# First loads of k, block sums and score order of a fused attention and expert kernel, rearranged

## The chip, the cores and the metric

The kernel runs on one core of a Trainium2 chip. The metric is device time in microseconds (us). Matrix products run on TensorE (PE in the profile, its weight loads PEld), elementwise work on VectorE (DVE) and ScalarE (ACT), loads with a cast and small memsets on GpSimd (POOL), stores and transposing DMAs are issued by SyncE (SP).

## The reference, cut to what matters

q, k and v are [4 batches, 8 heads, 768 positions, 64], all f32. Attention sees a window of 16 positions on either side, and beside it 24 blocks of 32 keys, each as one key (the maximum) and one value (the mean). What comes out is x [3072, 512] of a feed-forward layer with w_in [512, 2048] and w_out [2048, 512].

```
k_sum = k.reshape(B, H, nb, block, D).max(axis=3)
v_sum = v.reshape(B, H, nb, block, D).mean(axis=3)
scores_s = scale * einsum('bhsd,bhnd->bhsn', q, k_sum) + log(block)
scores_l = where(|i - j| < 16, scale * q @ k.T, -1e9)
a = softmax(concat([scores_l, scores_s]))
x = a @ concat([v, v_sum])
h = x @ w_in
out = (h * clip(h + 3, 0, 6) / 6) @ w_out
```

## The kernel before, in words

Products run in bf16. A batch's 768 positions are cut into 12 query tiles of 64, and each tile sees 96 window keys and the 24 block keys: 120 rows. The block maxima stand as columns WIN to KEYS of each key tile, the block sums of v as rows WIN to KEYS of each value tile (`vaug`). Heads go in four pairs, `p` or `c`. A batch has two halves of query tiles; half 0 is tiles 6 to 11. Each half becomes one tile `s` = 0 to 7 of the feed-forward layer, of 384 rows.

All work is written down as operations (`op`) with a name, an engine or a choice of engines, a cost, what they read and write, and a function that issues them. The string ORDER lists every operation in the order in which the plan places it, with the engine chosen (`:D` VectorE, `:A` ScalarE, `:P` GpSimd). `Plan.run` gives each a begin time by its costs, sorts by it and issues; so ORDER fixes the order of each engine's own queue. Names:

- K, Q, V, I, O: loads of k, q, v, w_in, w_out, all on GpSimd's queue, with the cast to bf16 in the DMA. For batch 0, `K01`, `K02`, `K00` are pair 1, pairs 2 and 3, pair 0 (L400); `Q00`, `Q01` the q of half 0, and `Q01w` that of half 1 (L419, L420).
- k0p (L510 to L545): .0 the TensorE transposes of pair p (L517), .1 VectorE's block maxima (L538), .2 and .3 the copies of the half 0 and half 1 key tiles out of PSUM, .4 the block columns (L544).
- q0p0, q0p1: transposes and copies of q; s0px: scores of pair p and half x (products L628, exp on ScalarE L637, mask product on VectorE L641). For half 0 the mask is added by a `cover` matmul instead (L617).
- h0cx: the halo, 32 rows of v copied beside each value tile (L464). u0c: block sums of pair c by 12 matmuls (L677) to a tile `vf`, .1 the copy out, .2 and .3 the spreads into `vaug` (L683).
- v00 to v02: values of half 0 by tile of 128 rows (L754 to L758), .2 and .3 the reciprocal (L833) and scaling (L837), .4 the transposes of x (L850), .5 their copy. v03: values of half 1 (L784 to L792), then transposes (L809) and copies.
- For batches 1 to 3: load_raw and VectorE's 32x32 transposes (batches 1, 2), load_nat and SP's transposing DMAs (batch 3); w: block maxima over a batch (L719); sb0 to sb5: scores of a sixth of the batch each (L658, L664, L666); ub: block sums of the batch by 48 matmuls (L694), a copy and eight spreads (L700); vb0, vb3: values of a half, after which a transposing DMA on SP's queue (L797) makes x.
- F: first feed-forward product (L868), relu6 (L874, L876); G: the second (L890), a copy and a store.
- c, z, e, f: constants (`idle`, identity `ident`, the masks `band`, `band3`, `bias`, `mask`, the indicator `ind`). `keep` (L980) fills TensorE's planned gaps early on with matmuls on `idle`.

GpSimd issues, before: K01, K02, Q01's first load, `band` (c.2), the other, `ident` (c.1), K00, three wide q loads, four v loads, then w_in with batch 1's k. SP's queue has nothing before the first stores and the first transposing DMA of batch 1.

Of the kernel before, what the change touches and what calls it, by code (L numbers as in the profile page):

```python
# [15 lines left out]
D = 64  # L16
# [13 lines left out]
K01.0 K02.0 Q010.0 c.2 Q000.0 c.1 K00.0 k01.0 c.0 e.4 z2.0:D c.9 e.1 f.0 e.2 c.4 c.7 c.8 e.0 k01.1 k01.3:D z0.0:A z1.0:A  # L30
k02.0 k02.2:A z3.0:A k01.2:A e.3 k02.1 q020.0 q030.0 s020.0 q020.1:D k03.0 q030.1:D k02.4 s020.1 k02.3:A s030.0 k00.0 q000.0
k03.1 k03.4 s020.2 k00.2:A k03.2:A k03.3:A Q01w0.0 Q01w2.0 Q01w1.0 q010.0 s030.1 k00.1 q010.1:D q011.0 q021.0 q000.1:D k01.4
s030.2 k00.3:A q011.1:A q021.1:D q031.0 q031.1:D s031.0 s031.1 V00.0 h001.0:D V02.0 c.3 c.5 s031.2 V01.0 s011.0 s021.0 s021.1
s011.1 V03.0 q001.0 s010.0 u02.0 u00.0 u02.1:A h020.0:A I0.0 h000.0:D k00.4 I2.0 K13.0 I3.0 K10.0 K11.0 K12.0 s010.1 s000.0
s010.2 q001.1:A s000.1 u01.0 s001.0 u01.1:A u02.2:D u00.1:D u00.2:D h010.0:D h030.0:D h011.0:D h021.0:D s021.2 h031.0:D
u01.3:D s011.2 s000.2 u01.2:A u03.0 u03.1:A s001.1 v00.0 v00.1 v00.2 u03.2:A u00.3:A v02.0 v02.1 v01.0 v01.1 v00.3 s001.2
v00.4 v01.2 v01.3 v03.3 v03.0 v02.2 v02.3 v03.1 v03.4 v03.2 v03.5 v00.5:A v01.4 v01.5:A F00.0 F00.1 v02.4 F00.2 F00.3 F00.8
F00.9 v02.5:A F00.4 v03.6 F00.5 F00.10 F00.11 F00.12 F00.6 F00.13 v03.7:D v03.8 F02.0 F00.14 F00.7 c.6:D F00.15 F02.1 F02.2
F02.3 F02.4 v03.9:A F02.5 v03.10 v03.11:D F02.6 F02.7 F03.4 F03.5 F03.6 F03.7 F10.0 F10.1 F12.4 F12.5 F10.2 F03.0 F03.1 F12.6
k13.0 F10.3 F12.7 F03.2 F12.0 F12.1 F13.4 F13.5 k11.0 F03.3 I1.0 O0.0 Q13.0 Q10.0 O1.0 Q12.0 Q11.0 O2.0 O3.0 V13.0 V12.0  # L40
V10.0 V11.0 F12.2 F13.6 F12.3 k12.0 F13.7 F10.4 F10.5 F10.6 k10.0 F10.7 F01.0 F01.1 F01.2 F01.3 w1.0 F01.4 G02.0 F01.5 F01.6
F11.4 F11.0 F11.1 F11.5 F01.7 w1.1 w1.4:A F11.6 F11.7 F11.2 F11.3 q11.0 q13.0 q12.0 q10.0 w1.3:A w1.2:A G01.0 G01.1 F13.0
# [27 lines left out]
G61.1 G61.2 G71.6 G71.9 G61.3 G71.10:D G71.1 G71.4 G71.7 G71.12 G61.4:D G71.11 G61.5 G71.13:A G71.14  # L70
"""

BANKS = ("S", "h")


SLOW = 5.8
# [155 lines left out]
def kernel(  # L232
# [161 lines left out]
    def low(x):  # L394

        return (1 - x) * HQ
# [629 lines left out]
```

## Time and profile before

| | us |
|---|---|
| median of 3 runs | 214.84 |
| lowest, highest | 214.73, 215.09 |
| the profiled execution's own time | 214.44 |
| its span | 212.7 |
| mean granted TensorE clock | 0.99 |

The span runs from the first to the last instruction of the profiled execution. "Busy" counts the time in which an engine has an instruction of its own in flight. A row such as `L538 DVE ... x4 | 3.8, 941 | 1.6 <-` reads: line 538, four instructions, 3.8 us busy, 941 ns each, 1.6 us idle ahead of them and what ended it. The chain of waits goes back from the last instruction: at each step to what released it. A merged row of the timeline (`x2`) gives the start of the first and the time to the end of the last.

### The profile page before, as it was taken

To read this page: it belongs to the slowest core of one execution; us is meant where nothing else is said; L and a number is where in the kernel's file an instruction comes from. 1 tells how busy PE (TensorE), PEld (TensorE's weight loads), DVE (VectorE), ACT (ScalarE), POOL (GpSimd) and SP (SyncE) were. 2 spreads that over 40 slices of the span, in tenths; PEclk is the share of its full clock that TensorE was granted. 3 is DMA by queue.
4 is the path that set the end of the run, shared out by engine and by line. 5 is a ranking of instruction groups with operands and counts; after the bars stand their busy time and mean duration, and the time that the engine had idled before them with its cause. 6 is when DMAs were issued, how large, how long until landed. Compare 5 with 4: busy or idle time off the path is not lost.

```text
span 212.7 us, 4928 instructions
## 1 busy us (share of the span) xinstructions
PE 205.3 (97%) x2105; PEld 116.8 (55%) x2105; DVE 149.8 (70%) x238; ACT 110.6 (52%) x157; POOL 66.9 (31%) x81
## 2 busy tenths in 40 slices
PE   7969999999999999999999999999999999999994
PEld 2447686655446555555555556555464555555462
DVE  5788988999978897898568679981874347542102
ACT  5478856658299036836893045669501246531120
POOL 7999247345420029945973000000000000000000
PEclk9988999999999999999999999999999999999999
DMA  4999999999999659999999999901109002000242
GB/s 64 184 157 194 179 135 177 147 149 184 151 115 47 176 123 103 143 210 153 162 148 143 136 190 171 208 0 52 51 3 197 0 3 99 0 0 3 99 159 89
DMA packets 121846, 25.01 MB, mean 118 GB/s; under 512 B 112864, under 2 KB 118880, under 8 KB 121824
## 3 DMA queue, kind: packets, MB, share of 16 engines
q0 software_dynamic: 102336, 14.47, 108.0%
q1 hardware_dynamic: 19488, 10.23, 20.4%
q8 instruction: 16, 0.26, 0.5%
q14 instruction: 6, 0.05, 0.1%
HBM read 28.93 MB, written 6.29 MB: 166 GB/s over the span
## 4 chain that ended last, share of the span: by engine, by line
PE 90%; DVE 6%; ACT 2%; issue 0%; ACTq 0%; DVEq 0%
PE S L868 39%; PE h L890 29%; PE S L890 11%; PE S L784 3%; PE h L983 2%; PE S L658 2%; DVE vaug L502 2%; ACT kb L502 1%; DVE xn L837 1%; DVE at L641 1%; DVE kb L544 1%; PE h L517 1%; PE S L694 1%; DVE q L502 1%; DVE red L538 0%
## 5 line engine op out<-in xcount | busy, mean ns | idle before, releaser
L868 PE MATMUL S<-x,win 128*128 128x384 bf16 (+1 forms) x544 | 88.3, 317 | 0.0
L874 ACT ACTIVATE r<-S 128x768 f32<-128x768 f32 x64 | 51.3, 811 | 67.2 <-PE S L868 65.6
L876 DVE SCALAR_TENSOR_TENSOR g<-r,S 128x768 bf16<-128x768 f32 x64 | 59.6, 948 | 26.8 <-ACT r L874 26.1
L868 PEld LDWEIGHTS <-win 128*128 128x128 bf16 x544 | 51.2, 98 | 34.8 <-issue 0.2
L890 PE MATMUL h<-wout,g 128*128 128x512 bf16 (+1 forms) x288 | 67.4, 370 | 0.0
L890 PEld LDWEIGHTS <-g 128*128 128x128 bf16 x416 | 38.4, 98 | 38.6
L890 PE MATMUL S<-wout,g 128*128 128x512 bf16 (+2 forms) x128 | 25.8, 346 | 0.0
L664 ACT ACTIVATE at<-S 120x1024 bf16<-120x1024 f32 x18 | 17.5, 1031 | 4.3 <-PE S L658 4.2
L453 POOL DMA_DIRECT2D vaug<-in_v_dram x16 | 15.2, 955 | 8.1 <-DMA wout<-in_moe_w_out_dram 4.3
L666 DVE TENSOR_TENSOR at<-at,mask 96x1024 bf16<-96x1024 bf16 x18 | 11.9, 685 | 7.4 <-ACT at L664 7.2
L442 POOL DMA_DIRECT2D nat<-in_q_dram x8 | 10.5, 1318 | 7.1 <-issue 7.1
L442 POOL DMA_DIRECT2D nat<-in_k_dram x8 | 10.7, 1348 | 5.0 <-issue 2.3
L502 ACT COPY ot<-h 128x512 f32<-128x512 f32 (+1 forms) x14 | 7.9, 567 | 7.3 <-PE h L890 5.2
L502 DVE COPY ot<-S 128x512 f32<-128x512 f32 (+2 forms) x6 | 3.5, 577 | 11.2 <-PE S L890 11.2
L719 DVE TENSOR_REDUCE red<-kb 128x48 bf16<-128x1536 bf16 x6 | 10.5, 1744 | 0.0
L502 DVE COPY vaug<-vs 24x768 bf16<-24x768 bf16 x17 | 6.0, 354 | 3.4 <-ACT vs L502 3.0
L784 PEld LDWEIGHTS <-at 120*64 120x64 bf16 x336 | 6.1, 111 | 2.7 <-issue 1.6
L983 PE MATMUL h<-g 128*128 128x512 bf16 x15 | 6.1, 566 | 1.5 <-DVE g L323 1.5
L792 DVE TENSOR_TENSOR xm<-S,rc 128x768 bf16<-128x768 f32 x8 | 7.5, 955 | 0.1
L596 DVE STREAM_TRANSPOSE kb<-nat 128x768 bf16<-128x768 bf16 x8 | 7.4, 957 | 0.0
L784 PE MATMUL S<-vaug,at 120*64 120x65 bf16 x336 | 7.0, 196 | 0.3 <-ACT vaug L502 0.3
L637 ACT ACTIVATE at<-S 120x768 bf16<-120x768 f32 x8 | 6.3, 818 | 1.8 <-PE S L628 1.7
(100 smaller groups left out, 161.4 us busy)
## 6 DMA issues: line engine op xcount, KB each, us to landing
out_dram<-ot SPq DMA_DIRECT2D x19, 256.0 KB, 2.5
vaug<-in_v_dram POOLq DMA_DIRECT2D x16, 192.0 KB, 8.0
win<-in_moe_w_in_dram POOLq DMA_DIRECT2D x4, 512.0 KB, 11.2
wout<-in_moe_w_out_dram POOLq DMA_DIRECT2D x4, 512.0 KB, 17.3
nat<-in_k_dram POOLq DMA_DIRECT2D x10, 192.0 KB, 13.1
nat<-in_q_dram POOLq DMA_DIRECT2D x10, 192.0 KB, 8.1
out_dram<-ot SPq DMA_DIRECT2D x4, 224.0 KB, 2.7
nat<-in_k_dram POOLq DMA_DIRECT2D x6, 128.0 KB, 7.0
```

What stands on the lines that cost most here:

```text
L442: op("POOL", 1.35, over=0.01, fn=lambda src=src, name=name, hs=hs, ds=ds, rows=rows: nc.gpsimd.dma_start(out=raw[b % 2][name][rows], in_=s ...
L453: op("POOL", 0.945, lambda: nc.gpsimd.dma_start(out=o[BLK:WIN, lo:hi, 0:D], in_=rows[:, lo:hi]), w=[("v", b % 2, c)], dma=1.28, els=1536)
L502: {"ACT": nc.scalar.copy, "DVE": nc.vector.tensor_copy, "POOL": nc.gpsimd.tensor_copy}[eng](o, i)
L664: op("ACT", 1.02, lambda: nc.scalar.activation(odds[0:KEYS, :, w], X.slot[0:KEYS], AF.Exp, scale=scl), r=[X], w=[("atg", k)])
L666: op("DVE", 0.69, lambda: nc.vector.tensor_tensor(odds[0:WIN, :, w].rearrange("p j (t c) -> p j t c", c=QB), odds[0:WIN, :, w].rearrange(" ...
L719: nc.vector.tensor_reduce(red.slot[:].rearrange("x (p u e n) -> x e u p n", p=NP, u=NS, e=2)[:, e], w[:, n * e:n * e + n, BLK:WIN].rearran ...
L784: nc.tensor.matmul(X.slot[64 * c:64 * c + 64, e, (D + 1) * y:(D + 1) * (y + 1)], at[p][0:KEYS, j, t * QB:(t + 1) * QB], vaug[b % 2][0:KEYS ...
L868: nc.tensor.matmul(h.slot[:, f, lo * 128:hi * 128].rearrange("p (u c) -> p u c", c=128), w_in_sb[:, kt, (ft + f) * 128:(ft + f + 1) * 128] ...
L874: op("ACT", 0.81, lambda: nc.scalar.activation(r.slot[:], h.slot[:, :, 0:HALF], AF.Relu, bias=0.5, scale=1.0 / 6.0), r=[h], w=[r], alloc=r)
L876: op("DVE", 0.955, lambda: nc.vector.scalar_tensor_tensor(gt[s].slot[:, ft:ft + 2], r.slot[:], 1.0, h.slot[:, :, 0:HALF], op0=ALU.min, op1 ...
L890: nc.tensor.matmul(bank(o)[:, a:z], gt[s].slot[:, ft, ts * 128:(ts + 1) * 128], w_out_sb[:, ft, a:z], start=(ft == 0), stop=(ft == NFT - 1))
L983: nc.tensor.matmul(o, idle[:, 0:128], idle[:], start=True, stop=True)
```

## The change

- K01 and K02 are issued on SP's queue as f32 into the space of a feed-forward tile, and rounded to bf16 by six copies C01, C02, C03 (.0 and .1, one per head) on ScalarE or VectorE. `band` and `ident` go ahead of GpSimd's loads, which now name `band` as something they read; the wide q loads come before K00.
- The block sums of batch 0 are made for two pairs at a time, (0, 2) and (1, 3), in two 32-row strips of one PSUM tile.
- The block sums of batch 3 no longer come from TensorE: v is loaded again in rows of one block each (`B3c`, four loads), and four VectorE reductions add 32 rows (`U3.0` to `.3`), a copy and the same eight spreads follow.
- A score group belongs to one half of the batch, and the values of a half wait for three groups, not six.
- x of half 1 of batch 1 (`v13`) goes by TensorE's transposes and three copies, as in batch 0, not by SP's transposing DMA.
- Halos and spreads may run on GpSimd: ORDER puts h020, h001, h030, h010, h031 and u02.1 there, and eight spreads and two halos of later batches. The block columns k0p.4 may run on ScalarE.
- The mask table gets eight more tiles, and its first part is shorter. Where the plan sees a gap of TensorE and no free PSUM, the `cover` matmul of half 0 is repeated.
- ORDER is new throughout. The head of it, and the part with batch 3's sums, are shown.

```
+K01.0 K02.0 c.2 c.1 Q010.0 Q000.0 Q01w2.0 Q01w1.0 Q01w0.0 c.0 z2.0:D e.1 f.0 c.9 e.3 c.7 c.4 C01.1:D e.2 C01.0:D c.8 z3.0:A
+z1.0:A z0.0:A k01.0 C02.1:A C02.0:A q030.0 q030.1:A C03.1:A K00.0 V02.0 V00.0 k02.0 s020.0 q020.0 k01.2:D C03.0:D k01.1 k02.1
+k01.4:D k01.3:A k03.0 q010.0 k03.2:A k02.2:A q010.1:A k02.3:A q020.1:D k03.1 k03.3:A k03.4:A q000.0 q000.1:D k02.4:D e.4
+q001.0 q031.0 q021.0 s020.1 q031.1:D q021.1:D e.0 s031.0 s020.2 s031.1 k00.0 s021.0 q011.0 q011.1:A s021.1 V03.0 V01.0
+q001.1:D k00.1 k00.2:D h021.0:D h000.0:D s011.0 s011.1 k00.4:A s030.0 s010.0 s030.1 s010.1 s000.0 s000.1 s030.2 s010.2 s000.2
+I0.0 I1.0 h020.0:P c.3 c.5 s031.2 s021.2 h001.0:P I3.0 h030.0:P I2.0 u00.0 u00.1:A u02.0:A k00.3:D s011.2 u00.2:D u00.3:D
+u01.0 s001.0 h010.0:P u02.1:P h031.0:P O0.0 K10.0 K12.0 K13.0 O2.0 K11.0 Q12.0 Q10.0 O1.0 Q11.0 Q13.0 u03.0:A u01.1:A s001.1
+u03.1:A h011.0:A u01.2:D u01.3:D s001.2 v00.0 v00.1 v01.0 v02.0 v01.1 v02.1 v00.2 v00.3 v00.4 v01.2 v01.3 v02.2 v02.3 v03.3
+v03.0 v03.1 v00.5:A v01.4 v01.5:D v02.4 F00.0 F00.1 F00.2 F00.3 v02.5:A F00.4 F00.5 v03.2 v03.6 v03.7:A F00.6 v03.4 v03.5
...
+F40.1 F23.2 F23.3 v23.4 v23.5 k3e1.0 q3x0.0 v23.6 q3x1.0 G31.5 G22.2 G20.3 F41.0 F43.4 F43.5 F40.2 G20.4:A F43.6 F40.3 U3.3
+G20.5 w3.1 F43.7 U3.2 w3.3:D F40.4 F41.1 F40.5 G21.0 w3.2:A F40.6 F41.2 F40.7 F41.3 F42.4 F42.5 F42.6 F42.7 w3.4:A G21.1
+G21.2 G21.3 s340.0 s340.1 s330.0 s350.0 G22.3 G21.4:A s350.1 F42.0 F42.1 U3.1 U3.4:A s330.1 F42.2 u3.2:A s330.2 u3.0:D F42.3
+F41.4 F41.5 F41.6 u3.5:P F41.7 G42.0 F43.0 F43.1 F43.2 s350.2 F43.3 F50.0 F50.1 F50.4 F50.2 F50.5 u3.6:A F50.6 F50.3 F52.4
+F52.5 F52.6 s340.2 F50.7 F52.7 G22.4:A G30.5 G21.5 G22.5 G42.1 G42.2 G42.3 s310.0 s300.0 s320.0 s320.1 G42.4:A s310.1 s300.1
+G40.0 G40.1 G40.2 F53.0 F51.4 s310.2 h30.0 V32.0 y10.0 h31.0 V33.0 V31.0 u3.3:P V30.0 h32.0 u3.7:P u3.1:P F53.1 F51.5 G41.0
+G41.1 G41.2 F53.2 F51.6 s300.2 F53.3 s320.2 u3.4:D F51.7 v33.0 v33.3 v30.0 G41.3 v33.1 v33.4 v33.2 v33.5 G41.4:D F53.4 F53.5
...
+    def load_wide_k(b, lo, hi):
+        plan.at(f"K{b}{lo}")
+        def raw_(p, n):
+            at_ = 2 * (p - 1) * RUN * D
+            return hards[0][0:RP].rearrange("p f c -> p (f c)").bitcast(F32)[:, at_:at_ + n * RUN * D].rearrange("p (h s d) -> p h s d", h=n, s=RUN)
+        op("SP", 0.4, lambda: nc.sync.dma_start(out=raw_(lo, 2 * (hi - lo)), in_=k[b, 2 * lo:2 * hi].rearrange("h (p s) d -> p h s d", s=RUN)),
+           w=[("kf", p) for p in range(lo, hi)], dma=0.95 * (hi - lo), kind="load")
+        for p in range(lo, hi):
+            plan.at(f"C{b}{p}")
+            for j in range(2):
+                op(EITHER, {"ACT": 0.59, "DVE": 0.68}, lambda eng, p=p, j=j: copy(eng, knat[:, 2 * p + j], raw_(p, 2)[:, j]),
+                   r=[("kf", p)], w=[("kn", p, j)])
...
     def scores_all(b, k):
-        X, n = Buf("S"), 8
-        of = sorted({i // NQ for i in range(n * k, n * k + n)})
+        X, n, half = Buf("S"), 8, 1 - k // 3
+        first = n * (k % 3)
+        of = sorted({i // HQ for i in range(first, first + n)})
...
+    def vsum_first(cs):
         T = Buf(("h", "S"))
         def mms():
             for t in range(NQ):
+                for i, c in enumerate(cs):
+                    nc.tensor.matmul(bank(T)[BLK * i:BLK * i + BLK, 0:2 * D], ind[:, t], vaug[0][0:WIN, 2 * c:2 * c + 2, t, 0:D],
+                                     start=(t == 0), stop=(t == NQ - 1))
...
+    def load_blocks(b, c):
+        plan.at(f"B{b}{c}")
+        op("POOL", 0.8, lambda: nc.gpsimd.dma_start(out=rows_v(b, c), in_=v[b, 2 * c:2 * c + 2].rearrange("h (n r) d -> n h (r d)", r=BLK)),
+           w=[("vb", b, c)], dma=0.95, els=192, free=[(n, 0, g) for n in ("Kr", "Qr") for g in range(4)])
+    def sum_blocks(b):
...
+                    x = both[0][:].rearrange("p u m -> p (u m)")[:, h * BLK * D:(h + 1) * BLK * D].rearrange("p (r d) -> p d r", r=BLK)
+                    nc.vector.tensor_reduce(total[:, h * D + lo:h * D + lo + n], x[:, lo:lo + n], axis=AX.X, op=ALU.add)
...
-            op("PE", 0.395, mms, form="values", r=([("atg", k) for k in range(6)] if b else [("at", p, half) for p in range(NP)])
+            op("PE", 0.395, mms, form="values", r=([("atg", 3 * (1 - half) + k) for k in range(3)] if b else [("at", p, half) for p in range(NP)])
...
-        if b:
+        if b > 1 or b and not half:
             op("SP", 1.3, lambda: nc.sync.dma_start(out=xt[s].slot[:].rearrange("p u k c -> p (u k) c"), in_=xm.slot[:], transpose=True),
...
+            elif o.again:
+                todo += [o.again] * int(max(o.begin - 0.15 - end, 0.0) / 0.33)
```

171 lines of the change are left out of this document (97 added, 74 removed).

## The prediction

> **What bounds the kernel now.** I read the page first (span, busy shares, the 40 slices), then the chain of waits, then the busy windows of the stages that the chain marks out.
>
> ```profile
> span 212.7 us, 4928 instructions
> ...
> PE 205.3 (97%) x2105; PEld 116.8 (55%) x2105; DVE 149.8 (70%) x238; ACT 110.6 (52%) x157; POOL 66.9 (31%) x81
> ...
> PE   7969999999999999999999999999999999999994
> ```
>
> TensorE (PE) is busy nearly everywhere; only the first slices and the last fall below 9. The chain says where it takes over:
>
> ```profile
> 28.14 0.15 DVE rc L791
> 28.29 0.60 PE S L868 x8
> ...
> 30.23 0.22 PE h L809 x4
> ...
> 95.92 0.86 PE h L890 x4
> 96.78 0.65 PE S L868 x4
> ...
> 117.44 0.78 PE S L694 x48
> ```
>
> ```profile
> 6.75:28.14 21.39, 18.56 (x385) 12.63 (x383) 19.47 (x46) 16.54 (x32) 17.30 (x20) 0.92 1.97 175
> 28.29:209.68 181.39, 181.37 (x1696) 102.12 (x1696) 126.71 (x176) 90.96 (x121) 44.21 (x47) 1.00 1.25 112
> 209.68:212.70 3.02, 0.00 (x0) 0.00 (x0) 0.00 (x0) 0.27 (x1) 0.00 (x0) 0.89 0.34 116
> ```
>
> The columns are the stretch, its length, the busy time of PE, PEld, DVE, ACT and POOL, the granted clock, the DMA share and GB/s. So there are three stages. The **head**, to 28.29 us, is batch 0's attention: VectorE is busy 19.47 of 21.39 us and ScalarE (ACT) 16.54, and TensorE waits for them. The **stream** is 181.39 us in which TensorE never stops; only TensorE work added, removed or starved counts there. The **tail** of 3.02 us is the last copy and store.
>
> The sum is made against the profiled execution: span 212.70, its own time 214.44, so 1.74 lies around the span. The median of the runs, 214.84, is 0.40 above that execution; I subtract differences from the median.
>
> **Stream.** Leaving out the block sums of batch 3 on TensorE removes one L694 group, 0.78 us. Turning x of half of batch 1 on TensorE adds three groups like L809's, 3 x 0.22 = 0.66. ORDER also puts the third x transposes of the first half (v02.4, now inside the stream, again 0.22 by L809's like) ahead of F00.0: 0.22 leaves the stream and enters the head. Stream: 181.39 - 0.78 + 0.66 - 0.22 = 181.05, a gain of 0.34. The pairwise sums of batch 0 issue the same 48 matmuls, in the head, where TensorE is not last; scores by halves issue the same 96 a batch. Both are worth nothing by themselves: they loosen what values must wait for. The x copies of that half (three, on ScalarE and VectorE, for one DMA transpose by SP) and the larger mask copy on ScalarE stand beside the stream, in which ScalarE is busy 91 of 181 us; they cost nothing. The repeated cover matmuls of the head only fill planned gaps of TensorE.
>
> What replaces the batch 3 sums is four VectorE reductions of 1024 elements a row. Nearest row:
>
> ```profile
> L719 DVE TENSOR_REDUCE red<-kb 128x48 bf16<-128x1536 bf16 x6 | 10.5, 1744 | 0.0
> ...
> L502 DVE COPY vaug<-vs 24x768 bf16<-24x768 bf16 x17 | 6.0, 354 | 3.4 <-ACT vs L502 3.0
> ```
>
> ```profile
> 122.70:143.00 20.30, 20.30 (x121) 11.55 (x118) 17.69 (x25) 12.24 (x16) 0.00 (x0) 1.00 0.78 142
> 143.00:160.00 17.00, 17.00 (x260) 9.49 (x260) 10.11 (x18) 8.29 (x10) 0.00 (x0) 1.00 0.09 33
> ```
>
> 1024/1536 of 1.744 is 1.16, times four 4.7 us; six of batch 3's eight spreads leave VectorE, 6 x 0.354 = 2.1. Net 2.6 us more, in two windows where VectorE idles 37.30 - 27.80 = 9.5 us under TensorE's stream: nothing. GpSimd (POOL) issues nothing there now and its DMA share is low, so the four block loads are hidden as well. If that cover went, each late us of VectorE would be one of TensorE.
>
> **Head, the start.** Pairs 1 to 3 of k now come by SP's queue as f32 and are cast by six copies, and the constants go ahead of GpSimd's loads.
>
> ```profile
> 5.38 0.29 POOL L318 TENSOR_SCALAR_AFFINE_SELECT ident<-ident 128x128 bf16<-128x128 bf16 x1
> ...
> 5.90 0.85 PE L517 MATMUL h<-ident,nat 96*64 96x96 bf16 x16
> ...
> 6.80 0.96 DVE L538 TENSOR_REDUCE red<-h 128x24 bf16<-128x768 bf16 x1 [0.72 <-PE h L517]
> ...
> 13.48 1.54 POOL L487 DMA_DIRECT2D win<-in_moe_w_in_dram  x2
> ```
>
> ```profile
> win<-in_moe_w_in_dram POOLq DMA_DIRECT2D x2, 512.0 KB, 9.3
> ...
> nat<-in_k_dram POOLq DMA_DIRECT2D x3, 192.0 KB, 5.0
> ```
>
> ```profile
> out_dram<-ot SPq DMA_DIRECT2D x19, 256.0 KB, 2.5
> ```
>
> ```profile
> SPq L1010 <- PEq L1010: 0.8, 1, 0.8
> ```
>
> ```profile
> L502 ACT COPY x<-h 128x512 bf16<-128x512 bf16 x2 | 1.2, 586 | 0.8 <-PE h L850 0.8
> ```
>
> The first k transposes start at 5.90, just after ident (5.67). Afterwards ident is early, and k waits for a load and two casts. SP is free at 0.8. No SP load stands in this trace; from issue to landing I bound it by SP's stores (2.5) and GpSimd's k loads (5.0): k lands at 3.3 to 5.8. A cast of 96x512 costs between 0.35 (the bf16 spread above) and 0.59 (ScalarE); I take 0.6, two make 1.2, and the transposes start at 4.5 to 7.0. The middle is today's start, so I take **no gain at the start**, 1.2 us either way. Nothing else is queued on SP then: its first store comes in the stream. The five early casts fall into time in which VectorE and ScalarE wait today.
>
> GpSimd's queue is reordered as well: the wide q loads go ahead of pair 0's k, and four halos stand between the chunks of w_in. Today the first chunk is issued at 13.48 and lands 9.3 us later, at 22.8; F00.0 needs it near 27, so up to 4 us of delay there are hidden. The other chunks follow it by the 2 us of two copies each, while F00 and F01 give TensorE over 5 us (eight groups of 0.65): hidden.
>
> **Head, VectorE's load** from its first reduction (6.80) to the third scaled tile (before the L791 that starts at 28.14), after which F00.0 starts:
>
> ```profile
> L538 DVE TENSOR_REDUCE red<-h 128x24 bf16<-128x768 bf16 x4 | 3.8, 941 | 1.6 <-ACT kb L502 0.9 <-PE h L517 0.7
> L502 DVE COPY q<-S 128x384 bf16<-128x384 bf16 x6 | 2.7, 485 | 0.1
> L544 DVE COPY kb<-red 128x288 bf16<-128x288 bf16 x4 | 2.6, 646 | 0.1
> L641 DVE TENSOR_TENSOR at<-at,mask 96x768 bf16<-96x768 bf16 x4 | 2.2, 552 | 0.4 <-ACT at L637 0.4
> L837 DVE TENSOR_TENSOR xn<-S,rc 128x512 bf16<-128x512 f32 x3 | 2.1, 692 | 0.1
> L502 DVE COPY vaug<-vaug 32x640 bf16<-32x640 bf16 x4 | 1.5, 380 | 0.0
> L502 DVE COPY vaug<-g 24x768 bf16<-24x768 bf16 x3 | 1.5, 484 | 0.1
> L502 DVE COPY vaug<-vaug 32x768 bf16<-32x768 bf16 x3 | 1.2, 412 | 0.0
> ...
> L502 DVE COPY kb<-h 128x480 bf16<-128x480 bf16 x1 | 0.6, 648 | 0.0
> ```
>
> These rows and the small ones between (short halos 0.7, two small k copies 0.4, mask 0.7, reciprocals 0.6, a cast 0.3, a memset 0.1) add to 21.0 us, and the stretch took 21.3: overlaps and waits nearly cancel. The new ORDER gives VectorE, from k01.2 to v02.3: four maxima 3.76, one cast 0.6, two first-half k copies and one second-half (0.75 + 0.75 + 0.9) 2.4, two block columns 1.29, five q copies 2.43, two memsets 0.3, two halos 0.96, the shorter mask 0.4, four mask products 2.2, four spreads 1.94, three scalings with reciprocals 2.7: **19.0 us, 2.1 less**. Out are four halos and a spread (to GpSimd), one halo and some copies (to ScalarE); in are k copies and a cast. ScalarE's own list comes out about even: three casts (1.8) and a halo for two long k copies, one halo, two spreads and a tile copy.
>
> The 2.1 us is an upper end. Two equally loaded engines hand work to each other more often, and v00.0 now also waits for halos from GpSimd's queue, behind its loads; I charge 0.9, within bounds of 0 and 2.1. VectorE's end: 28.1 - 1.2 = 26.9. Then F00.0 waits for v02.4 (0.22 and a handover), 27.3 against 28.29: a **head gain of 1.0**.
>
> Sum: 1.0 + 0.34 = 1.3 us. Span 211.4, and **214.84 - 1.3 = 213.5 us**.
>
> **GpSimd's copies.** Six copies of the head move there: five halos and a spread. No GpSimd copy of that size stands in the trace; 0.36 to 0.83 (VectorE, ScalarE) bound one, and I take 0.83, 5 us in all. The trace shows what GpSimd does to VectorE:
>
> ```profile
> 15.16 0.23 DVE L544 COPY kb<-red 128x288 bf16<-128x288 bf16 x1
> ...
> 18.64 1.16 DVE L544 COPY kb<-red 128x288 bf16<-128x288 bf16 x1
> ```
>
> ```profile
> L442 POOL DMA_DIRECT2D nat<-in_k_dram x4 | 5.4, 1380 | 0.0
> ```
>
> One and the same copy took 0.23 us and 1.16, both beside GpSimd's issuing. The means above hold this loss already (0.646 against 0.23 four times is 1.7 us). The six copies displace 5.4 us of L442 issuing (it stands at 15 to 21 us now), so I charge nothing more; the other end is that every GpSimd copy holds VectorE up for its whole length, 5 us.
>
> [...]
>
> **Rivals.**
> - *The copies collide.* VectorE's mask products, halos and spreads stand exactly beside GpSimd's six copies. If each GpSimd copy holds VectorE for half its length, 6 x 0.42 = 2.5 us more: 214.84 - 1.3 + 2.5 = **216.0**. It turns the sign beyond 0.22 us a copy. For it: 1.16 against 0.23. Against: equal GpSimd work stands there now. [...]
> - *The head stays as long.* k lands late (5.0 rather than 2.5 us) and the casts stand on the way, or GpSimd's halos come late: the head gain is 0 and **214.5** is left.
> - *Batch 3 comes late.* Its v loads now queue on GpSimd behind a spread that needs all four reductions. Twelve instructions there, at the 0.83 taken above, are 10 us, against some 20 us of stream work that ORDER puts between (16 groups of 0.65, 10 of 0.86). Were VectorE 12 us late, TensorE would stop for 2: **215.5**.
> - *All of it counts.* k lands at 3.3 and waits do not grow: 2.1 + 0.34 and 0.2 at the start: **212.2**.
>
> **How the numbers follow.** Forecast (212.9 to 214.4) 0.45; more 0.16; head as long, 0.14; collision 0.16; batch 3 or another bubble 0.09. About 0.2%, 0.43 us, is what can be told from no change here. Faster 0.61, same 0.14, slower 0.25. The range runs from the large gain to the collision: 212.0 to 216.2.
>
> **What would show it.** F00.0 (first L868) near 27.3; the first L517 between 4.5 and 7; TensorE full from F00.0 to the end in about 181 us; no L694 group in batch 3; four reductions near 1.16 us. Wrong, if halos or mask products on VectorE in the head take much over 0.36 and 0.55 us, if SP's first load lands after 5.8, or if TensorE idles at batch 3's values.

## The result, and the profile after

The changed kernel takes 217.06 us (median of 4 runs, 216.84 to 217.39) against 214.80 (4 runs, 214.73 to 215.09): a ratio of 1.0104, interval 1.0086 to 1.0121. It is 1% slower, where 213.5 was forecast, and lies above the range. The profiled execution took 217.04 us, 2.60 more than the one of before (214.44), and its span is 2.62 longer: 215.33 against 212.71.

The page of the changed kernel, the same lines as of before:

```profile
span 215.3 us, 4890 instructions
...
PE 202.9 (94%) x2071; PEld 114.8 (53%) x2071; DVE 155.5 (72%) x225; ACT 112.7 (52%) x165; POOL 81.6 (38%) x102
...
PE   7869799999997999999899999999999999999992
```

The row of TensorE has a 7 and an 8 in the middle, in the slices from 64.6 and from 102.3 us: TensorE, which never stopped there before, now waits. The busy windows by the same three stages, with the columns of the prediction:

```profile
6.75:26.98 20.23, 16.11 (x389) 10.75 (x387) 18.21 (x40) 15.87 (x35) 16.79 (x24) 1.00 1.72 186
26.98:211.47 184.49, 181.58 (x1659) 102.10 (x1656) 132.55 (x169) 92.97 (x125) 58.83 (x65) 1.00 1.31 112
211.47:215.33 3.86, 0.00 (x0) 0.00 (x0) 0.00 (x0) 0.27 (x1) 0.00 (x0) 0.82 0.25 87
```

The head ends at 26.98 and not at 28.29, 1.31 us earlier. The stream takes 184.49 us and not 181.39, 3.10 more, with TensorE busy for 181.58 of it. The tail takes 3.86 and not 3.02. Together -1.31 + 3.10 + 0.84 = 2.63, the whole difference. So the gain came in the head, where most of it was forecast, and the loss in the stream, which was forecast 0.34 shorter, and in the tail, which was to stay as it was. TensorE's waits in the stream of the changed kernel, of which the kernel before has none:

```profile
PE h L753 <- ACT ot L528: 1.4, 1, 1.4
PE S L688 <- DVE g L941: 0.6, 1, 0.6
PE S L688 <- ACT kb L528: 0.5, 1, 0.5
PE S L849 <- DVE at L696: 0.3, 1, 0.3
PE S L874 <- DVE qwide L857: 0.2, 1, 0.2
```

The rows are ordered by length; in order of time the waits stand at 66, 70, 75, 106 and 130 us (1.35, 0.33, 0.15, 0.58 and 0.47). Each costs more than its idle time. The wait at 106 has 0.58 us of idle time, yet the groups of scores around it start 0.75 us later than their undisturbed distance; undisturbed, a group starts a little before the one ahead of it has ended (one of 0.87 us is followed after 0.81).

**The wait at 66 us** is for room to write to. The chain of waits there:

```profile
59.95 1.09 ACT ot L528 x2
...
61.05 4.65 DMA out_dram<-ot
...
65.80 0.59 ACT ot L528
...
66.44 0.88 PE h L753 x48
```

Output tiles leave PSUM through three `ot` buffers. The new ORDER finishes four tiles close together (G02, G01, G11, G10), and the first store took 4.65 us to land. ScalarE's copy of the fourth tile waits for that, and TensorE's block sums of batch 1 (L753) wait for the bank that this copy frees. Before, three such copies stood at 60 to 69 us and a fourth at 74.

**The wait at 106 us** comes from VectorE. Its timeline in the changed kernel, and then GpSimd's:

```profile
101.66 0.69 DVE L696 TENSOR_TENSOR at<-at,mask 96x1024 bf16<-96x1024 bf16 x1 [2.11 <-ACT at L694]
102.36 2.17 DVE L528 COPY vaug<-vs 24x768 bf16<-24x768 bf16 x3
104.57 0.69 DVE L696 TENSOR_TENSOR at<-at,mask 96x1024 bf16<-96x1024 bf16 x1
105.18 0.94 DVE L941 SCALAR_TENSOR_TENSOR g<-r,S 128x768 bf16<-128x768 f32 x1
```

```profile
102.60 1.72 POOL L528 COPY vaug<-vs 24x768 bf16<-24x768 bf16 x2
```

Three spreads took 2.17 us where one took 0.354 before (the row L502 of the prediction); two of them came while a GpSimd copy was running and took 0.88 each. The product at 105.18, which frees TensorE's next bank, stands behind them.

**The wait at 130 us** is for ScalarE's copy of k; the theory is that a VectorE that is full holds it up. VectorE's groups in the stream:

```profile
L740 DVE TENSOR_REDUCE total<-nat 128x32 f32<-128x1024 bf16 x4 | 7.7, 1918 | 0.0
...
L528 DVE COPY vaug<-vs 24x768 bf16<-24x768 bf16 x9 | 5.5, 611 | 0.2
```

A reduction takes 1.918 us, not the 1.16 of the forecast, and a spread 0.611 in the mean, not 0.354. What the waits at 70 and 75 us come from was not taken apart.

**The tail.** SP's waits at the end, first before and then after:

```profile
SPq L1021 <- DMA out_dram<-ot: 0.5, 2, 0.3
```

```profile
SPq L1094 <- DMA out_dram<-ot: 1.3, 1, 1.3
```

Before, SP waits for the two last stores last. After, one wait ends it, and others still follow. The trace's record of SP's closing instructions shows why (start in us; the semaphores each waits for):

```
before                              after
210.78 wait 115, 100                212.16 wait 112, 111
211.25 wait 116, 99                 213.47 wait 101, 110  <- last store landed at 213.46
211.59 wait 117, 107                213.53 wait 104, 109
211.79 wait 118, 109  <- 211.78     213.60 wait 113, 108
211.87 drain                        213.69 wait 114, 107
                                    213.77 wait 115, 106
                                    214.26 wait 116, 105
                                    214.34 wait 117, 100
                                    214.40 wait 118, 103
                                    214.48 drain
```

SP's transfers use eight semaphores in turn (111 to 118 before; 101, 104 and 113 to 118 after), and in both traces the closing waits go through these in the same order. With 40 transfers the last one falls on the last semaphore; with 41 it falls on the first, and seven waits come behind its landing: 1.02 us from landing to drain in place of 0.09. Of the 1.02, 0.48 is a single pause ahead of the wait for 116; before, a pause of 0.48 at the same place passed while the last stores were still under way.

### The profile page after: what moved, and what is told of

Same layout as the page of the kernel before. It is cut to its first block, busy times and chain, and to the rows that moved or that the text cites. A ratio compares the mean times of both kernels' runs of the same rounds, so it can differ in the third digit from the quotient of the medians.

```text
span 215.3 us, 4890 instructions
## 1 busy us (share of the span) xinstructions
PE 202.9 (94%) x2071; PEld 114.8 (53%) x2071; DVE 155.5 (72%) x225; ACT 112.7 (52%) x165; POOL 81.6 (38%) x102
## 4 chain that ended last, share of the span: by engine, by line
PE 69%; DVE 17%; DMA 5%; ACT 4%; issue 1%; SPq 0%; DVEq 0%; ACTq 0%
PE S L933 33%; PE h L955 22%; PE S L955 8%; DVE vaug L528 4%; DMA g<-in_k_dram 3%; DVE total L740 2%; DVE g L941 2%; DMA out_dram<-ot 2%; PE S L849 2%; DVE at L696 2%; DVE qwide L857 2%; ACT kb L528 2%; DVE red L783 2%; PE S L688 1%; ACT ot L528 1%
## 5 line engine op out<-in xcount | busy, mean ns | idle before, releaser
L941 DVE SCALAR_TENSOR_TENSOR g<-r,S 128x768 bf16<-128x768 f32 x64 | 59.9, 948 | 27.3 <-ACT r L939 26.8
L939 ACT ACTIVATE r<-S 128x768 f32<-128x768 f32 x64 | 51.3, 811 | 51.0 <-PE S L933 48.2
L955 PE MATMUL h<-wout,g 128*128 128x512 bf16 (+2 forms) x336 | 73.3, 359 | 0.0
L528 POOL COPY vaug<-vs 24x768 bf16<-24x768 bf16 x8 | 6.8, 847 | 35.4 <-ACT vs L528 32.4
L955 PE MATMUL S<-wout,g 128*128 128x512 bf16 x80 | 18.4, 379 | 0.0
L528 ACT COPY ot<-h 128x512 f32<-128x512 f32 (+1 forms) x16 | 9.0, 565 | 16.1 <-DMA out_dram<-ot 13.4
L528 POOL COPY vaug<-vaug 32x640 bf16<-32x640 bf16 (+2 forms) x11 | 6.6, 614 | 7.0 <-DMA vaug<-in_v_dram 3.9
L1054 PE MATMUL h<-g 128*128 128x512 bf16 x21 | 7.3, 497 | 1.5 <-DVE g L328 1.5
L528 ACT COPY ot<-S 128x512 f32<-128x512 f32 x3 | 1.7, 589 | 12.7 <-PE S L955 12.7
L740 DVE TENSOR_REDUCE total<-nat 128x32 f32<-128x1024 bf16 x4 | 7.7, 1918 | 0.0
```

Of the source, the lines that this page charges most:

```text
L528: {"ACT": nc.scalar.copy, "DVE": nc.vector.tensor_copy, "POOL": nc.gpsimd.tensor_copy}[eng](o, i)
L740: nc.vector.tensor_reduce(total[:, h * D + lo:h * D + lo + n], x[:, lo:lo + n], axis=AX.X, op=ALU.add)
L939: op("ACT", 0.81, lambda: nc.scalar.activation(r.slot[:], h.slot[:, :, 0:HALF], AF.Relu, bias=0.5, scale=1.0 / 6.0), r=[h], w=[r], alloc=r)
L941: op("DVE", 0.955, lambda: nc.vector.scalar_tensor_tensor(gt[s].slot[:, ft:ft + 2], r.slot[:], 1.0, h.slot[:, :, 0:HALF], op0=ALU.min, op1 ...
L955: nc.tensor.matmul(bank(o)[:, a:z], gt[s].slot[:, ft, ts * 128:(ts + 1) * 128], w_out_sb[:, ft, a:z], start=(ft == 0), stop=(ft == NFT - 1))
```

## The experiments

The theory: the head gained what was forecast, and the loss is in places that can be repaired one by one (the stores, VectorE beside GpSimd, the reductions, SP's closing waits). The rival: the new order is simply fuller, and a wait taken away comes back at the next place.

The table reads from each profile the start of the first relu6 activation (L939; it marks the end of the head), the time from there to the end of the last output copy (the **way**, which a disturbance of the head doesn't touch), and the time from there to the end. The medians are from several chips; the kernel before had 214.5 to 214.8 beside all of them. The changed kernel itself has 217.06 and 218.10, so single medians don't tell one edit from another. Nor is the way exact: in the five profiles whose stream no edit aimed at (changed, after_again, no_gpsimd_copies, tail_lane, k_gpsimd) it is 182.27 to 182.95 us, and the wait at 66 us, in the nine profiles that leave its cause alone, is 1.09 to 1.64 us.

| kernel | first relu6 | way | end | median us |
|---|---|---|---|---|
| before | 30.71 | 179.30 | 2.70 | 214.80 |
| changed | 29.23 | 182.53 | 3.58 | 217.06 |
| after_again | 29.59 | 182.38 | 3.57 | 218.10 |
| ot_stores | 30.08 | 181.59 | 3.58 | 217.22 |
| red_tree | 29.99 | 181.54 | 3.56 | 216.81 |
| u2_later | 29.88 | 181.97 | 3.56 | 217.32 |
| g12_early | 30.34 | 182.79 | 3.57 | 217.83 |
| sums_te | 29.42 | 184.37 | 3.56 | 219.37 |
| no_late_gpsimd | 31.00 | 188.82 | 3.56 | 225.08 |
| no_gpsimd_copies | 31.84 | 182.27 | 3.56 | 218.88 |
| k_gpsimd | 30.42 | 182.95 | 3.25 | 218.38 |
| tail_lane | 31.63 | 182.43 | 2.63 | 216.44 |
| best | 29.39 | 180.65 | 2.63 | 215.66 |
| best2 | 29.82 | 180.64 | 2.63 | 215.07 |

**after_again**, the changed kernel itself as the measure on the chip of three others.

> The changed kernel itself, beside the others on their chip. Both theories: 217.0 +-0.4 us, first feed-forward matmul at 27.0 us, TensorE's waits behind it 2.9 us in all (1.35, 0.33, 0.15, 0.58, 0.47), 3.8 us from TensorE's last matmul to the end. If that first matmul comes at 27.8 us here, as it did with the stores moved, then 0.8 us of that run belongs to the chip or to the execution and not to the edit.

Measured: 218.10 us (217.27 to 219.72, 5 runs; ratio 1.0173, 1.0128 to 1.0218), the way as before within 0.15. The five waits of the changed kernel stand at the same places (1.19, 0.33, 0.15, 0.58 and 0.49 in order of time). The median lies above the 217.0 +-0.4 that was expected, and the first feed-forward matmul, expected at 27.0 us, came at 27.34. What differs from execution to execution is the head, by the granted clock. The stretches 11.4 to 14.8, 14.9 to 18.2 and 18.3 to 21.7 us of this kernel, and then the second of them of the first profile of the changed kernel (the last three columns are the granted clock, the DMA share and GB/s):

```profile
11.40:14.80 3.40, 2.14 (x63) 1.64 (x60) 2.70 (x8) 3.40 (x11) 2.26 (x4) 1.00 2.12 167
14.90:18.20 3.30, 3.30 (x36) 1.32 (x28) 3.13 (x8) 2.75 (x5) 2.35 (x7) 0.50 2.17 172
18.30:21.70 3.40, 3.40 (x100) 2.32 (x96) 3.14 (x8) 2.84 (x6) 1.69 (x3) 1.00 1.24 207
```

```profile
14.90:18.20 3.30, 3.16 (x72) 1.70 (x63) 3.14 (x7) 3.26 (x7) 3.16 (x8) 1.00 2.13 174
```

From 14.86 us on TensorE ran at half its clock for 3.41 us; 36 matmuls fill the stretch in which the other execution did 72. The first profile of the changed kernel has no such stretch in its head; that of before has one (a mean of 0.57 from 14 to 18 us). So the head's 1.31 us compares unlike executions: with one stretch in each, the first feed-forward matmul comes here at 27.34 us in place of 28.29, a gain of 0.95. The heads of ot_stores, red_tree, u2_later, g12_early, sums_te and best have the same instructions in the same order on VectorE, ScalarE and GpSimd, and one stretch each that begins between 13.6 and 15.4 us. Together with after_again their first feed-forward matmul comes at 27.15 to 28.09 us, 27.57 in the mean: like for like the head's gain is 0.2 to 1.1 us, 0.7 in the mean, against the one profile of before.

**ot_stores**: the stores of the three tiles right behind their copies in ORDER.

```
-G02.4:A G11.3 V10.0 ... G01.4:A G11.4:A ... G01.5 G10.4:A G10.5 G02.5 G11.5
+G02.4:A G02.5 G11.3 V10.0 ... G01.4:A G01.5 G11.4:A G11.5 ... G10.4:A G10.5
```

> The changed kernel, with one edit: the stores of the first three output tiles stand in SP's queue in the order of their copies, ahead of the store of the fourth. Theory A (three separate losses in the stream and the tail): in the changed kernel SP's second store waits for the fourth tile's copy, and that copy waits on ScalarE for the first store, so two full tiles sit unsent; with the edit ScalarE's 1.52 us of waiting at 64 us and TensorE's 1.35 us before the block sums of batch 1 go, and the time falls by 1.0 to 1.5 us, to about 215.8. Rival B (GpSimd's copies block VectorE, and that is the loss): the stop before the block sums only changes its name, less than 0.3 us is gained.

Measured: 217.22 us (216.69 to 219.10), ratio 1.0104 (1.0028 to 1.0180). The wait at 66 fell from 1.35 us to 0.41:

```profile
PE h L753 <- ACT ot L528: 0.4, 1, 0.4
```

The way became 0.87 us shorter, yet the profiled end didn't move, since the first feed-forward matmul came at 27.84 us, with a half-clock stretch in the head. The first store still took 4.2 us to land, which is why 0.41 is left. The mechanism is shown, since 0.41 is far below the 1.09 to 1.64 us of the profiles without this edit; the time gained can only be read from the way.

**g12_early**: four matmuls that need no new bank ahead of the waiting sums.

```
-u1.0 u1.1:D ... h20.0 Q20.0 G12.1 G00.0
+G12.1 u1.0 u1.1:D ... h20.0 Q20.0 G00.0
```

> Four matmuls of tile G12 (0.87 us, into a bank that it holds already) stand ahead of the block sums of batch 1 on TensorE and not behind the next scores. Theory A (TensorE waits there for a bank that ScalarE's late copy of an output tile holds, and nothing else is late): the wait of 1.2 to 1.35 us at 66 falls by 0.87, and the next 0.33 at 70 doesn't grow; from the first feed-forward matmul to the last copy 0.9 us less than in the changed kernel (184.4 to 183.5). Theory B (it comes back at the next wait): the wait at 70 grows by as much, 184.4.

Measured: 217.83 us (217.23 to 219.96), ratio 1.0172 (1.0133 to 1.0211); the way 0.33 us longer, which is within the scatter of the profiles without an edit there. The waits tell more, and by them the rival is right:

```profile
PE S L849 <- DVE at L696: 0.7, 1, 0.7
PE h L753 <- ACT ot L528: 0.7, 1, 0.7
...
PE h L955 <- DVE vs L528: 0.5, 1, 0.5
```

The wait at 66 halved, the one at the values of batch 1 rose from 0.33 to 0.68, and a new one of 0.46 stands between them: after the sums there is a chain of copy, spreads, masks and values, and what holds up its start is paid at its end.

**u2_later**: VectorE's three spreads of batch 2 behind two masks and a product.

```
-u2.0 u2.1:A s240.0 s240.1 s240.2 u2.4:D u2.2:D u2.6:D K35.0 ... s250.2 G30.1
+u2.0 u2.1:A s240.0 s240.1 s240.2 K35.0 ... s250.2 u2.4:D u2.2:D u2.6:D G30.1
```

> VectorE's three spreads of batch 2's sums stand behind two masks and a product of the feed-forward part, not ahead of them, so that they no longer run beside GpSimd's copies ahead of what TensorE waits for. Theory A (two of the three take 0.88 us beside GpSimd's copies in place of 0.35, and that makes TensorE wait 0.58 us at 106): the spreads take 0.35 each, the wait at 106 goes, and 0.5 us less from the first feed-forward matmul to the last copy (184.4 to 183.9). Theory B (VectorE is full there from 99 to 131 whatever the order): the wait turns up at the values of batch 2 or at 130, 184.4.

Measured: 217.32 us (216.41 to 217.60), ratio 1.0123 (1.0106 to 1.0140); the way 0.49 us shorter (of the mean of the two profiles of the changed kernel, 182.45). The same three spreads, no longer beside GpSimd's:

```profile
106.21 1.08 DVE L528 COPY vaug<-vs 24x768 bf16<-24x768 bf16 x3
```

0.36 each. The wait at 106 is gone; 0.28 us came back at a feed-forward matmul at 115 us. The wait at 106 therefore came from these spreads standing there, beside GpSimd's and ahead of the product; the edit moves them in the queue as well, so it doesn't price the collision apart from the place.

**red_tree**: the sums of batch 3 as additions of halves.

```
-                    x = both[0][:]...rearrange("p (r d) -> p d r", r=BLK)
-                    nc.vector.tensor_reduce(total[:, ...], x[:, lo:lo + n], axis=AX.X, op=ALU.add)
+                    while m >= (BLK * D // 2 if lo == 0 else D):
+                        nc.vector.tensor_tensor(total[:, h * D:h * D + D] if m == D else x[:, 0:m], x[:, 0:m], x[:, m:2 * m], op=ALU.add)
+                        m //= 2
```

> The block sums of batch 3 on VectorE as a tree of additions, each half as long as the one before (per pair of heads one of 1024 elements, then 512, 256, 128 and 64), in place of four strided reductions at 1.92 us. Theory A (the reductions' length keeps VectorE full and makes ScalarE's copy of k, and so TensorE, late at 130 us): 2 x (0.7 + 0.8) = 3.0 us in place of 7.7, the wait of 0.47 us at 130 gone, 216.6 us. Theory B (a wait taken away there comes back at the next): no change, 217.0 us.

Measured: 216.81 us (216.57 to 218.44), ratio 1.0119 (1.0083 to 1.0155), beside 218.10 of after_again on its chip; the way 0.91 us shorter, more than the wait of 0.47 that went: with its edges that wait cost 0.65, and the wait at 66, ahead of the edited place, happened to be 1.11 us here and not 1.35 or 1.19. The additions, by size:

```profile
L742 DVE TENSOR_TENSOR nat<-nat 128x1024 bf16<-128x1024 bf16 x2 | 1.4, 684 | 0.0
...
L742 DVE TENSOR_TENSOR nat<-nat 128x512 bf16<-128x512 bf16 x2 | 0.8, 418 | 0.0
L742 DVE TENSOR_TENSOR nat<-nat 128x256 bf16<-128x256 bf16 x2 | 0.6, 292 | 0.1
L742 DVE TENSOR_TENSOR nat<-nat 128x128 bf16<-128x128 bf16 x2 | 0.5, 226 | 0.1
L742 DVE TENSOR_TENSOR total<-nat 128x64 f32<-128x64 bf16 x2 | 0.5, 226 | 0.1
```

3.7 us (twice 1.846) in place of 7.7, and not the 3.0 expected, for the same sums but for their rounding. The wait at 130 is gone and none came in its place, so the theory holds here.

**sums_te**: the sums of batch 3 on TensorE again, as before the change; the block loads and reductions are gone.

```
-        if b < 3:
+        if b < 4:
             vsum(b)
-u3.2:A u3.0:D ... u3.3:P u3.7:P u3.1:P ... u3.4:D
+G40.2 u3.0 u3.1:A u3.5:D u3.3:D u3.9:D u3.7:D ... u3.4:D u3.8:D u3.2:D u3.6:D v33.0
```

> The changed kernel, with the block sums of batch 3 on TensorE again (48 matmuls, one copy, eight spreads on VectorE after the v loads; no second load of v, no VectorE reductions). Theory A: the four reductions measured 1.92 us each, not the 1.16 that was estimated, and they stand in a stretch in which VectorE has no room; without them TensorE's stops of 0.58 and 0.47 us between 104 and 131 us go, 0.78 us of matmuls come back: net gain 0.0 to 0.4 us. Rival C (the reductions cost more than the stops show, since the scores of batch 3 start late and work is pushed behind them): a gain of 1 us or more. If the reductions were harmless: 0.8 us slower.

Measured: 219.37 us (218.95 to 219.83), ratio 1.0193 (1.0118 to 1.0268); the way 1.92 us longer, which none of the three expectations had. The wait at 130 went, as the theory has it, but the one at 106 didn't: it grew (0.58 to 0.93). 0.78 us of matmuls came back, and the eight spreads, put late, made TensorE wait in the middle of the values:

```profile
PE S L688 <- DVE g L941: 0.9, 1, 0.9
PE S L849 <- DVE vaug L528: 0.5, 1, 0.5
```

The last one is of this experiment's own making, so it doesn't price the old sums in the new order. What made the wait at 106 grow is a mask product on VectorE, 1.18 us here and 0.69 in the changed kernel (101.66 us above). It began while GpSimd was copying, which it did not there:

```profile
102.00 1.18 DVE L696 TENSOR_TENSOR at<-at,mask 96x1024 bf16<-96x1024 bf16 x1 [2.11 <-ACT at L694]
```

```profile
100.95 2.93 POOL L528 COPY vaug<-vs 24x768 bf16<-24x768 bf16 x3 [9.16 <-ACT vs L528]
```

What taking these sums off TensorE is worth by itself is not measured; the 0.78 us of matmuls is its price on TensorE alone, and red_tree shows that the strided form of the reductions gave about that much back.

**no_late_gpsimd**: the copies of batches 1 to 3 away from GpSimd.

```
-h121.0:P h131.0:P u1.5:P u2.8:P u2.5:P u2.9:P u3.5:P u3.3:P u3.7:P u3.1:P
+h121.0:D h131.0:D u1.5:A u2.8:A u2.5:A u2.9:A u3.5:A u3.3:A u3.7:A u3.1:A
```

> The copies of batches 1 to 3 that GpSimd makes are ScalarE's (spreads) and VectorE's (two pairs of halo copies of batch 1) again; GpSimd keeps only those of the head. Theory A (VectorE's copies beside GpSimd's take 0.72 to 0.88 us in place of 0.36 to 0.42 and make the masks late): VectorE's spreads at 67 and 102 us at 0.36 to 0.42 us, TensorE's waits of 0.33 us at 70 and 0.58 us at 106 gone, 216.2 us. Theory B (each copy on ScalarE takes 0.83 us there, and what stands behind it comes late): 217.0 to 217.6 us.

Measured: 225.08 us (223.01 to 225.72), ratio 1.0467 (1.0420 to 1.0513). Far worse than either theory had it. ScalarE's groups from 60 to 135 us:

```profile
L694 ACT ACTIVATE at<-S 120x1024 bf16<-120x1024 f32 x12 | 11.6, 1033 | 0.1
L528 ACT COPY vaug<-vs 24x768 bf16<-24x768 bf16 x9 | 7.5, 828 | 1.5 <-DVE vs L528 1.3
```

Nine spreads of 0.828 us stand in ScalarE's queue there (six in the changed kernel, in the same time), three of them between one exponential and the next (104.34 to 106.85 us); scores, masks and values follow late, and the way grows by 6.4 us. A half-clock stretch from 111.3 to 114.7 us (eight matmuls of the second feed-forward product take 3.25 us there and 1.89 at 105.8) is part of that, at most 1.7 us. So with the rest of ORDER as it is, these copies cost far more on ScalarE and VectorE than their collisions do on GpSimd. An order made for ScalarE's copies was not tried. For the spreads of batch 2, u2_later shows the cheaper way: what has to move is the VectorE work beside them.

**no_gpsimd_copies**: the six copies of the head away from GpSimd.

```
-h020.0:P h001.0:P h030.0:P h010.0:P u02.1:P h031.0:P
+h020.0:A h001.0:D h030.0:D h010.0:D u02.1:D h031.0:D
```

> The changed kernel, with the six copies that GpSimd makes in the head given back: one halo to ScalarE, four halos and a spread to VectorE. Rival B (collision): VectorE's spreads fall from 0.82 to about 0.36 us each and the first feed-forward matmul starts 1 us or more earlier than 27.0, total about 216.0. Theory A: VectorE takes back about 2.0 us of copies and loses 1.9 us of blocking, so the start moves by less than 0.5 us either way and the total stays within 0.5 us of 217.1.

Measured: 218.88 us (218.24 to 220.40), ratio 1.0175 (1.0101 to 1.0250). The first feed-forward matmul comes at 29.59 us against 27.34 in after_again, each with one half-clock stretch at 15 to 18 us, and later than in any of the seven like heads above; the way is the same. The plan also put more matmuls on `idle` into the longer gaps: eight run to 25.58 us, and the values begin right behind them, so how much of the 2.25 us is VectorE's longer list and how much is these matmuls is not told apart. Either way the rival of the prediction that the copies collide is right about the collision and wrong about its price. VectorE's spreads in the head, in the changed kernel and then in this one:

```profile
L528 DVE COPY vaug<-g 24x768 bf16<-24x768 bf16 x4 | 3.1, 821 | 0.0
```

```profile
L528 DVE COPY vaug<-g 24x768 bf16<-24x768 bf16 x5 | 2.4, 520 | 1.1 <-ACT g L528 1.0
```

**k_gpsimd**: pairs 1 to 3 of k by GpSimd's queue with its cast, ahead of the constants, as before.

```
-K01.0 K02.0 c.2 c.1 Q010.0 ... C01.1:D ... C01.0:D ... C02.1:A C02.0:A ... C03.1:A ... C03.0:D
+K01.0 K02.0 c.2 c.1 Q010.0 ...
-    load_wide_k(0, 1, 2)
+    load_k(0, 1, 2)
-    load_wide_k(0, 2, 4)
+    load_k(0, 2, 4)
```

> The changed kernel, with pairs 1 to 3 of k loaded by GpSimd's queue with the cast in the DMA, ahead of the constants, and no cast copies (the rest of the order as it is; q then comes about 1.4 us later). If SP's loads with casts gain: the first feed-forward matmul starts later than 27.0, at about 28, total near 218. If the casts only eat what the earlier start gives (the second load landed at 7.85, the casts ended at 9.0): start between 26.5 and 27.5, total within 0.5 us of 217.1.

Measured: 218.38 us (218.32 to 219.41), ratio 1.0153 (1.0089 to 1.0218). By the numbers the first expectation came out (first feed-forward matmul at 27.94 us), but a half-clock stretch from 25.0 to 28.4 us stands ahead of that matmul. Up to there the head is early: the first k transposes start at 5.03 us and not at 5.83, and the values of half 0 go on at 22.89 us and not at 23.27 (both executions at full clock up to 25 us), so nothing in this pair shows a gain from the load by SP. SP's first load landed at 4.56 us and the second, with pairs 2 and 3, at 7.83. The way is 0.5 us longer, with 1.6 us of wait at 68, where a store took 5.12 us to land:

```profile
62.24 5.12 DMA out_dram<-ot
```

**tail_lane**: one store of 16 rows by GpSimd's queue, so that SP issues 40 transfers.

```
-                    nc.sync.dma_start(out=out[(b + 1) * S - n:(b + 1) * S, a:z], in_=ot.slot[0:n, a:z])
+                    (nc.gpsimd if (b, a) == (2, 0) and n else nc.sync).dma_start(out=out[(b + 1) * S - n:(b + 1) * S, a:z], in_=ot.slot[0:n, a:z])
```

> One store of 16 rows of a tile of the third batch goes by GpSimd's queue, so that SP issues 40 transfers and not 41, as in the kernel before, and its last store falls on the last of the eight semaphores that SP waits for at the end. Theory A (SP's closing waits stand in a fixed order of semaphores; in the changed kernel the last store's semaphore is the first of eight, and seven waits of 0.07 to 0.5 us come behind its landing): 1.02 us from the last landing to SP's drain falls to 0.1, the end 2.9 us behind TensorE's last matmul and not 3.8, 216.1 us. Rival (the stores land later, or the end's code is fetched later, whatever the semaphore): 3.8 us, 217.0 us.

Measured: 216.44 us (216.30 to 218.40, 6 runs), ratio 1.0083 (1.0060 to 1.0106). Its tail by the busy windows:

```profile
213.76:216.69 2.93, 0.00 (x0) 0.00 (x0) 0.00 (x0) 0.27 (x1) 0.00 (x0) 1.00 0.33 115
```

2.93 us as expected, in place of 3.86, with the drain 0.08 us behind the last landing. The theory of SP's closing waits is shown; the median fell by more (218.10 to 216.44 on one chip) than the 0.93 us of the tail, which the heads' scatter allows. This execution also has the longest head of an unchanged order, the first feed-forward matmul at 29.16 us, with half-clock stretches at 12.6 to 19.4 and 26.2 to 29.6 us.

**best and best2**: all of it (ot_stores, u2_later, red_tree, tail_lane), once with the four matmuls of G12 ahead and once without.

> All that was found, in one: stores behind their copies, G12's matmuls ahead, the spreads of batch 2 later, the sums of batch 3 as a tree, 40 transfers on SP's queue. Theory A (the changed kernel lost its time to those places, and what is left of the change is a gain): from 217.1 to 218.1 us less 0.8 (stores and matmuls; 1.2 if both add up), 0.5, 0.8 and 0.94: 214.0 to 215.0 us, against 214.7 of the kernel before. Theory B (each wait comes back elsewhere): 216.2 us, as with the transfers on SP's queue alone.

> The version of all repairs without the four matmuls of G12 ahead: those made the way from the first feed-forward matmul to the last copy 0.40 us longer when they were moved alone. Theory A (they take TensorE's place ahead of the sums, which the spreads, masks and values of batch 1 wait for): 0.4 us less than with them, 182.1 us on that way, 214.0 us in the best executions against 214.4 of the kernel before, and a median of 215.2 with those in which the granted clock dips inside the head. Theory B (with the stores early they cost nothing): the same as with them, 214.4 at best and 215.7 in the median.

Measured: best 215.66 us (214.38 to 216.46, 6 runs), ratio 1.0059 (1.0039 to 1.0079); best2 215.07 us (214.09 to 217.16, 12 runs) beside 214.73 of the kernel before (17 runs), ratio 1.0006 (0.9970 to 1.0041). The way is 180.65 and 180.64 us, 1.8 less than in the changed kernel, where the three gains one by one add up to 2.27: 0.5 us came back, about as much as the scatter of the way. By the way G12's matmuls cost nothing once the stores are early, as the second theory on best2 has it; its median of 215.7 did not come, 215.07 is nearer the first's 215.2, on another chip. What is left in best2:

```profile
PE h L756 <- DVE at L696: 0.6, 1, 0.6
PE S L852 <- DVE at L696: 0.3, 1, 0.3
PE S L688 <- ACT ot L528: 0.2, 1, 0.2
```

The median of best lies between its two theories (214.0 to 215.0, and 216.2). The repairs give the loss back; none of these versions is shown to beat the kernel before.

## Why the prediction was wrong, point by point

- **The head gain of 1.0**: right within the scatter. The first feed-forward matmul was forecast at 27.3 us and stood at 26.98 without a half-clock stretch, and at 27.15 to 28.09 with one as in the profile of before. VectorE's busy time fell from 19.47 to 18.21 us, 1.26 and not the 2.1 counted, so what came true is the 1.2 that was left after the charge of 0.9. The start gave nothing, as forecast (first transposes at 5.83 us), though the forecast counted with one landing of k and there are two, at 4.56 and 7.83 us. Its 9.3 us for w_in is the median of two chunks: the first landed at 21.67 us, not 22.8, which changes nothing.
- **GpSimd's copies charged at nothing**: wrong by itself. A spread on VectorE took 0.353 us alone and 0.87 to 0.99 when a GpSimd copy of that size was running as it came. In the head four of them took 0.821 in the mean: 1.9 us more than alone, 1.3 more than the 1.94 that the forecast put down. That the forecast of the head still came out is partly luck, a charge of 0.9 for waits that was not made for this. The loss that the prediction read beside GpSimd's issuing (0.23 and 1.16 us for one and the same copy) is there beside GpSimd's own copies too, and the mask products have it as well (0.55 us alone, 0.95 beside them in after_again).
- **The stream's gain of 0.34**: this is the step that failed. Its sum of matmuls was right: 184.49 less what the five waits cost by the starts of the groups around them (1.42, 0.52, 0.43, 0.75 and 0.65 us) is 180.7, against 181.05. What failed is that the kernel before's full TensorE (181.37 of 181.39 us) was carried over to a new ORDER, with no term for waits: the changed ORDER brings five, 2.9 us of idle time and 3.8 with their edges.
- **"Both are worth nothing by themselves"**, of pairwise sums and scores by halves, and spreads and halos of later batches on GpSimd passed over: what was left out is their ORDER. Scores by halves and pairwise sums were not tried alone, so nothing shows them to cost or gain by themselves; but the ORDER that came with them crowds four tile copies onto three buffers (1.42 us) and GpSimd's copies onto VectorE's spreads ahead of scores (0.75).
- **The reductions, "nothing"**: mis-sized and mis-placed. 1.918 us each in place of 1.16, so 5.6 us net and not 2.6, and not in the 9.5 us where VectorE idles: they run from 112.6 to 132.2 us, in a stretch where VectorE is busy 28.18 of 31.60 us. The estimate took its price for one element from a maximum over runs of 32 neighbours; these are sums of elements that lie 64 apart. Which of the two differences costs the time was not tried. The wait at 130 that goes with them cost 0.65 us.
- **The tail unchanged**: the second step that failed, by 0.84 us, by something that no forecast case had: the number of SP's transfers (41 in place of 40, and 1.02 us in place of 0.09 from the last landing to the drain).
- **The rivals**: the collision gave 216.0 and the right sign, but for a place, the head, where the gain outweighed it. "Batch 3 comes late" named a bubble of TensorE and put it at the values; TensorE has no wait there, and the bubbles were elsewhere. The range ended at 216.2, since it held one mishap at a time; five waits and the tail came together.

What stays open: in best2 the way is still 1.3 us longer than before. Its stream takes 182.59 us, 1.9 more than the 180.7 that the matmuls alone would take; four waits leave TensorE idle for 1.3 us of that, and that the rest is their edges is only argued. Nor is it shown that the new head's executions spread more. On one chip best took 214.38 to 216.46 us in 6 runs and the kernel before 214.36 to 214.69 in 11; on another best2 took 214.09 to 217.16 in 12 and the kernel before 214.36 to 217.29 in 17. The half-clock stretches have a part in it: one and the same head ended at 26.98 us with none of them and at 29.16 in tail_lane, with stretches at 12.6 to 19.4 and from 26.2 us on. But with single stretches that begin within 2 us of each other it ended anywhere from 27.15 to 28.09, and why was not tried.

## What to carry to other kernels

Where one engine is full, a reordering is not priced by summing that engine's work: follow the buffers of each group (which copy frees its bank, which store frees that copy's buffer, what stands ahead on the copying engine) through the new order. Work moved to an idle GpSimd was not free here where VectorE's copies (0.87 to 0.99 us in place of 0.353) and mask products (1.18 in place of 0.69) ran beside it ahead of something that TensorE needed; moving the neighbour (u2_later) did better than moving the work back (no_late_gpsimd). Count the transfers on a queue whose end the program waits for (41 on SP's queue ended 0.93 us later than 40).

## What the runs showed of the hardware that was not expected

- The closing waits of SP cost 0.06 to 0.10 us each, in the order of eight semaphores, and one pause of 0.47 to 0.48 us was seen among them: 1.02 us behind the last landing with 41 transfers, 0.08 to 0.09 with 40. With 39 (k_gpsimd) the end lies between: 3.25 us from the last output copy, where it is 3.56 to 3.58 in the other versions of the changed kernel with 41 and 2.63 in those with 40.
- A VectorE copy of 24x768 in bf16 took 0.353 us alone and 0.87 to 0.99 when a GpSimd copy of that size was already running. When VectorE's copy began first, it took its 0.353 and GpSimd's 1.006 in place of 0.82 (67.7 us in the changed kernel). Beside GpSimd's issuing of DMAs it took 0.36 (19.83 us in the kernel before) or 0.74 (69.02 us in the changed kernel), and three in a row took 2.18 (from 69.36 us in no_late_gpsimd).
- VectorE's mask products took longer behind GpSimd's copies too. Of 96x1024 elements they took 0.62 to 0.69 us, beside GpSimd's issuing of DMAs as well, and 1.18 behind a GpSimd copy (sums_te). Of 96x768 they took 0.55, and 0.95 in the head of after_again, behind the copies that its second line shows:

```profile
23.57 0.95 DVE L669 TENSOR_TENSOR at<-at,mask 96x768 bf16<-96x768 bf16 x1
```

```profile
23.38 1.30 POOL L528 COPY vaug<-vaug 32x640 bf16<-32x640 bf16 x2
```

- A VectorE sum of 1024 bf16 elements that lie 64 apart took 1.918 us, a maximum of 1536 that lie in runs of at least 32 took 1.74, and the same sum as a tree of additions 0.92 per 1024.
- TensorE's clock halved for 3.41 us or twice that in the head of 13 of the 14 profiled executions: in nine once, beginning between 13.6 and 15.4 us, in the others at 11.2, at 12.6 and 26.2, at 25.0 and at 26.0 us. Through such a stretch the granted clock was 0.50 (14.04 to 17.45 us in the kernel before). In the 3.41 us before these stretches TensorE was busy for 1.9 to 2.9 us (2.00 in the kernel before). What starts a stretch, and why the moments differ from run to run, was not shown.
